# The second FFN product in 20 block products over 4 x 3 x 2 blocks in place of 21 over 2 x 2 x 2

## The chip, the cores and the metric

The kernel runs on one core of a Trainium2 chip, as one program in one launch. Five engines take part, each with its own queue of instructions: TensorE (PE, whose weight loads are shown apart as PEld), VectorE (DVE), ScalarE (ACT), GpSimd (POOL, which does next to nothing here) and SyncE (SP, which issues nearly all DMAs). The metric is the time of the launch on the device in microseconds (us), the median of several runs.

## What is computed

Attention with a sigmoid in place of a softmax, for 8 batches, 12 heads, 448 positions and heads of 64, then a feed-forward network of two products on the joined heads:

```
scores = q @ k.T / sqrt(64) - log(448)
attn   = 1 / (1 + exp(-scores)) @ v            # 8 x 12 x 448 x 64
x      = attn, heads joined                     # 3584 x 768
h      = x @ w_in                               # 3584 x 2048
g      = max(0.01 * h, h)
out    = g @ w_out                              # 3584 x 768
```

All values are float32.

## The kernel before

Rows of x belong to a batch, 448 (S) to each, and two batches (2p and 2p+1) make a pass p; there are four passes (NQ). Results are held transposed: features on the 128 partitions, the 448 positions of one batch along them. Every product of the FFN is done in three matmuls: each operand is split into a high part, which ScalarE rounds to the type that TensorE takes (`copy` into an F32R tile), and a low part, the rest, which VectorE subtracts (`sub`); high x high, high x low and low x high are added up in PSUM.

The work runs in three stages. The first is attention, two heads (a `Pair`) at a time. In it and in the first product a generator, `prep` (line 270), gets the two weight matrices ready on VectorE, a few steps at a time as `prepare(pace)` (line 330) calls for, by the numbers in `PACES` (line 28): it decodes the numbers that come in as int64, forms sums of blocks and stores the results in DRAM tiles `td`. The second stage is the first FFN product (`First`, line 561; slots of nine matmuls, 1.8 us each), the third the second FFN product (the loop at line 795).

Both FFN products use a scheme for 2x2 blocks with seven block products in place of eight: the blocks of the left operand (two batches by two halves of the features) and of the weights (two by two) are added and subtracted beforehand, and each of the seven products (`ORDER`, line 20) goes into one or more of four results. `Quad` (line 158) holds the accumulators and says when one is read out. For the second product the left operands are made at the end of the first: `First.after` (line 586) applies the slope (`leaky`), forms the sums of the four blocks on VectorE (`sums`, three new tiles and one in place for each u, that is, for each of 8 pairs of feature blocks) and stores all seven operands to the DRAM tiles `gd` (`save`).

In the second product the loop runs over items: pass p, product n, and pairs of u (`KS` = 2), so 4 x 7 x 4 = 112 items of 18 matmuls (3 blocks of output columns, 2 u, 3 parts). For item k, in one slot: the weights' tiles, if some are still to be made (load in slot k, high part one slot on, low part two slots on); `g_load(k + 3)`, one DMA of 448 KB; `g_high(k + 2)` on ScalarE; `g_low(k + 2)` on VectorE; and the 18 matmuls of item k. Three buffers hold loaded operands (`gp`, tag `g`) and three the split ones (tag `gs`). Chores that are due (`later`) are issued ahead of the slot's own work: reading an accumulator of a product that has just ended (`collect`, line 789), and the stores of outputs one slot later. The weights' tiles (`Weights`, line 122) are split once, seven of them ahead of the stage (`AHEAD`) and 25 in its first 27 slots; later passes use them again.

The order of the work is written out by hand: `pinned` (line 83) keeps every matmul, DMA, ScalarE and VectorE instruction that goes through it in the order of the program on its queue. The lines that carry it:

```python
def pinned(issue):
    return lambda *args, **kw: tc.keep_in_program_order(issue(*args, **kw))
...
            g_load(k + 3)
            g_high(k + 2)
            g_low(k + 2)
            x = gs.pop(k)[1]
```

In the profile all pinned instructions have line 85, so groups are told apart by their tiles: `px_o`, `py_o`, `pz_o` are accumulators of the second product, `px_h` and so on those of the first, `gg` a loaded operand, `gs` a split one, `wx` and `w` a weight tile before and after its split, `c_o` and `c_h` results, `wd` and `ws` decoded weights and their sums.

Of the kernel before, what the change touches and what calls it, by code (L numbers as in the profile page):

```python
# [25 lines left out]
AHEAD = 7  # L26

PACES = (4, 5, 4.2, 2.8, 2), 2
# [5 lines left out]
LEFT, MORE, RIGHT = 8, 6, 14  # L34

# [16 lines left out]
def attn_ffn_kernel(ctx: ExitStack, tc: tile.TileContext, qk, v, w_in, w_out, out):  # L52
# [21 lines left out]
    NQ = B // 2  # L74
    scale = 1.0 / math.sqrt(D)
# [3 lines left out]
    td = [[tc.dram_tile([P, NOP, HW], F32, name=f"t{w}_{u}") for u in range(NU)] for w in range(2)]  # L79
    xd = [tc.dram_tile([P, NB, S], F32, name=f"xd_{n}") for n in range(4)]  # L80
    gd = [[tc.dram_tile([P, NU, S], F32, name=f"g_{p}_{n}") for n in range(NOP)] for p in range(NQ)]
# [10 lines left out]
    def sub(to, x, y):  # L92
        vec(out=to, in0=x, in1=y, op=ALU.subtract)
# [24 lines left out]
    stage = ctx.enter_context(tc.tile_pool(name="stage", bufs=3))  # L118
# [3 lines left out]
    class Weights:  # L122


        def __init__(self, w, u, g, pool, tag, bufs=None, src=None):
            self.w, self.u, self.g, self.n = w, u, g, len(GROUPS[g])
            self.to = pool, tag, bufs
            self.src, self.stage = src, stage

        def load(self):  # L130
            name = f"wx{self.w}_{self.u}_{self.g}"
            if self.src is None:
                x = self.stage.tile([P, 2, HW], F32, tag="stage", name=name)
            else:
                x = self.src(name).rearrange("p a b -> p (a b)")[:, :2 * HW].rearrange("p (a b) -> p a b", a=2)
            self.x = x[:, :self.n]
            assert (self.w, self.u) in prepared
            dma(out=self.x, in_=td[self.w][self.u][:, PLACES[self.g]])

        def high(self):  # L140
            pool, tag, bufs = self.to
            t = pool.tile([P, 1 if tag == "t1" else 2, 2, HW], F32R, tag=tag, name=f"w{self.w}_{self.u}_{self.g}", bufs=bufs)
            self.t = t[:, :self.n]
            copy(out=self.t[:, :, 0], in_=self.x)
# [4 lines left out]
        def of(self, n):  # L149
            return self.t[:, GROUPS[self.g].index(n)]  # L150

# [68 lines left out]
    left, right = ExitStack(), ExitStack()  # L220

# [47 lines left out]

    def prep():  # L270
# [22 lines left out]
        for at, (m, k) in enumerate(pieces):  # L293
# [22 lines left out]
            dma(out=td[w][u][:, :3], in_=dec[:, 1:])  # L316

            b12, b22, b11, b21 = (dec[:, i] for i in range(4))
            sums = block(F32, (4, HW), f"ws{w}_{u}")
            for to, x, y in ((2, b12, b11), (0, b22, sums[:, 2]), (1, b22, b12), (3, b21, sums[:, 0])):  # L320
                sub(sums[:, to], x, y)
                yield
            dma(out=td[w][u][:, 3:], in_=sums)
# [208 lines left out]
    for p in range(NQ):  # L532
        for u in range(NU):
            for g, members in enumerate(GROUPS):
                w1.append((NOP * (p * NU + u) + ORDER.index(members[0]), Weights(0, u, g, ring, "ring")))
# [25 lines left out]
    class First:  # L561
# [24 lines left out]
        def after(self, quad, c, u, n):  # L586
            got = quad.done(n)
            if got is None:
                return
            p = self.p  # L590
            row, col, t = got
            c[row, col] = t

            def save(n, t):
                dma(out=gd[p][n][:, u], in_=t)

            def sums(n, fn, x, y):
                c[n] = st.tile([P, S], F32, tag="st", name=f"s{n}_{p}_{u}", bufs=ST)
                fn(c[n], c[x], c[y])

            if n != 2:
                later(1, lambda: leaky(t, t))
            if n == 1:
                later(3, lambda: save(0, t))
            elif n == 3:
                later(3, lambda: save(6, t))
            elif n == 6:

                z = LATER if u == NU - 1 else 0
                later(2, lambda: sums(3, add, (1, 0), (1, 1)))  # L610
                later(3 + z, lambda: sums(4, sub, 3, (0, 0)))
                later(4, lambda: save(3, c[3]))
                later(4 + z, lambda: sub(t, c[0, 0], t))
                later(5 + z, lambda: save(4, c[4]))
                later(6 + z, lambda: save(5, t))
            else:
                z = LATER if u == NU - 1 else 0
                later(2, lambda: save(1, t))
                later(4 + z, lambda: sums(2, sub, (0, 1), 4))
                later(6 + z, lambda: save(2, c[2]))  # L620
# [95 lines left out]
    assert next(preps, None) is None  # L716
# [11 lines left out]
    def g_tile(name):  # L728
        return gp.tile([P, KS, S], F32, tag="g", name=name)

    items = [(p, n, u0) for p in range(NQ) for n in ORDER for u0 in range(0, NU, KS)]
    gs = {}

    def g_load(k):
        if k < len(items):
            p, n, u0 = items[k]
            gs[k] = [g_tile(f"gg{p}_{n}_{u0}")]
            dma(out=gs[k][0], in_=gd[p][n][:, u0:u0 + KS])

    def g_high(k):  # L740
        if k < len(items):
            gs[k].append(gp.tile([P, 2, KS, S], F32R, tag="gs", name="gs{}_{}_{}".format(*items[k])))
            copy(out=gs[k][1][:, 0], in_=gs[k][0])

    def g_low(k):
        if k < len(items):
            sub(gs[k][1][:, 1], gs[k][0], gs[k][1][:, 0])

    use = [(g, u) for g in range(len(GROUPS)) for u in range(NU)]
    w2 = {(g, u): Weights(1, u, g, t2a, "t2", None, g_tile) for g, u in use[:AHEAD]}  # L750

    for k in range(NOP, size):
# [8 lines left out]
        if rest == 3:  # L761
            later(0, lambda: g_high(0))
        elif rest == 2:
            later(0, lambda: g_low(0), lambda: g_high(1))
        elif rest == 1:
            later(0, lambda: g_low(1))
        if rest in (7, 6, 5):
            later(0, lambda r=rest: g_load(7 - r))
# [7 lines left out]
    op = ctx.enter_context(tc.tile_pool(name="op", bufs=8, reuse_waits="tile"))  # L776
    t2b = ctx.enter_context(tc.tile_pool(name="t2b", bufs=len(use) - NU - AHEAD - len(GROUPS), reuse_waits="tile"))
    for i, (g, u) in enumerate(use[AHEAD:]):
        one = len(GROUPS[g]) == 1
        pool, tag = (ring, "ring") if i < len(GROUPS) else (t2b, "t1" if one else "t2")  # L780
        w2[g, u] = Weights(1, u, g, pool, tag, NU if one else None)
    psum = banks("ps_o", dict(px=(3, 1), pz=(5, 1)))

    def store(p, m, got):
        row, col, t = got
        b = 2 * p + row
        dma(out=out[col * NB + m, :, b * S:(b + 1) * S], in_=t)

    def collect(p, n, quads):
        for m, x in enumerate(quads):  # L790
            got = x.done(n)
            if got is not None:
                later(1, lambda m=m, got=got: store(p, m, got))

    for k, (p, n, u0) in enumerate(items):
        if u0 == 0:
            if n == ORDER[0]:
                quads = [Quad(psum, op, "o", f"o{p}_{m}", 8) for m in range(NB)]
            accs = [x.into(n) for x in quads]
        g = next(g for g, members in enumerate(GROUPS) if n in members)  # L800
        ending = k == len(items) - 1

        def work():
            for i, step in ((k, "load"), (k - 1, "high"), (k - 2, "low")):
                if 0 <= i < len(use) - AHEAD:
                    getattr(w2[use[AHEAD + i]], step)()
            g_load(k + 3)
            g_high(k + 2)
            g_low(k + 2)
            x = gs.pop(k)[1]  # L810
            for m, (acc, begins) in enumerate(accs):
                for e in range(KS):
                    u = u0 + e
                    parts_mm(acc, w2[g, u].of(n), slice(m * P, m * P + P), x[:, 0, e], x[:, 1, e], begins and u == 0, u == NU - 1)
                if ending and m < NB - 1:
                    store(p, m, quads[m].done(n))
                elif ending:

                    t = op.tile([P, S], F32, tag="o", name="end", bufs=8)
                    b = 2 * p  # L820
                    for cols, how, queue in zip(HALVES, (copy, vcopy), (dma, dma_act)):
                        how(out=t[:, cols], in_=acc[:, cols])
                        queue(out=out[NB + m, :, b * S + cols.start:b * S + cols.stop], in_=t[:, cols])
# [46 lines left out]
```

## Time and profile before

| what | value |
|---|---|
| time of the runs (3) | median 1063.91 us, 1062.86 to 1064.01 |
| time of the profiled execution | 1063.13 us, its span 1061.3 us |
| attention | about 0 to 251 us |
| first FFN product | about 251 to 654 us |
| second FFN product | about 654 to 1058 us |
| granted clock of TensorE | 1.00 |
| HBM | 167.38 MB read, 87.16 MB written |

The profile is of one execution. Its times count from the first instruction, so the time of a launch is somewhat above the span. A busy share is the part of the span in which an engine works on an instruction; waiting at the head of its queue isn't counted. A group of instructions shows what it writes and reads (out<-in), its shape as partitions x elements, how many there are, their busy time and the mean ns of one, and then how long the engine had been idle just before them and what ended the wait. In the order of time a row starts with the start and the duration in us; a wait is put in brackets at its end. Matmuls of 128x448 are listed with some 362 ns because they overlap; what counts is the distance between them.

### The profile page before, as it was taken

How to read it: one execution, taken by the hardware profiler on the slowest of the kernel's cores; microseconds unless marked ns; L12 is line 12 of the kernel's file. 1: busy time of each engine (PE TensorE's matmuls, PEld its weight loads, DVE VectorE, ACT ScalarE, POOL GpSimd, SP SyncE). 2: the span in 40 equal slices, each digit the busy share in tenths (PEclk: the TensorE clock that was granted, in tenths of full speed). 3: DMA queues.
4: the chain of work that ended last, by engine and by line, in shares of the span. 5: the costliest groups of instructions: out<-in, count | busy, mean ns of one | idle time of the engine just before them, and what ended most of it. 6: DMA issues, size and time to landing. Idle time of an engine off the chain costs nothing.

```text
span 1061.3 us, 16140 instructions
## 1 busy us (share of the span) xinstructions
PE 1055.8 (99%) x5882; PEld 889.0 (84%) x5882; DVE 684.2 (64%) x1045; ACT 569.9 (54%) x809; POOL 0.3 (0%) x5
## 2 busy tenths in 40 slices
PE   9999999999999999999999999999999999999998
PEld 5555545557999999998999999999999999999997
DVE  5778989877896898788976666655333433332332
ACT  6877778776555655555565555553323233323331
POOL 0000000000000000000000000000000000000000
PEclk9999999999999999999999999999999999999999
DMA  7878888898798888889788787866554554454542
GB/s 265 284 290 272 289 290 273 281 364 273 229 316 285 242 277 284 299 283 355 241 283 287 256 274 266 319 232 223 169 160 125 178 157 152 130 183 148 160 152 87
DMA packets 107935, 255.61 MB, mean 241 GB/s; under 512 B 11984, under 2 KB 55888, under 8 KB 107856
## 3 DMA queue, kind: packets, MB, share of 16 engines
q1 hardware_dynamic: 107280, 254.02, 72.4%
q8 instruction: 46, 0.75, 0.3%
q10 hardware_dynamic: 576, 0.57, 0.2%
q14 instruction: 33, 0.27, 0.1%
HBM read 167.38 MB, written 87.16 MB: 240 GB/s over the span
## 4 chain that ended last, share of the span: by engine, by line
PE 53%; DVE 0%; ACT 0%; issue 0%
PE px_o L85 22%; PE pz_o L85 11%; PE px_h L85 8%; PE py_o L85 5%; PE pz_h L85 4%; PE py_h L85 2%; DVE end L85 0%; ACT end L85 0%
## 5 line engine op out<-in xcount | busy, mean ns | idle before, releaser
L85 DVE TENSOR_TENSOR gs<-gg,gs 128x896 fp32r<-128x896 f32 x112 | 122.3, 1092 | 226.8 <-ACT gs L85 226.8
L85 PE MATMUL px_o<-gs,w 128*128 128x448 f32 x1152 | 232.5, 362 | 0.0
L85 PE MATMUL px_h<-hi,w 128*128 128x448 f32 x768 | 231.4, 362 | 0.9 <-DVE w L85 0.8
L85 PEld LDWEIGHTS px_o<-gs,w 128*128 128x128 f32 x1152 | 216.0, 187 | 14.4
L85 ACT CAST gs<-gg 128x896 fp32r<-128x896 f32 x112 | 105.3, 941 | 224.4 <-PE px_o L85 116.4
L85 PEld LDWEIGHTS px_h<-hi,w 128*128 128x128 f32 x768 | 143.7, 187 | 11.5 <-DVE w L85 1.6
L85 PE MATMUL px_h<-lo,w 128*128 128x448 f32 x384 | 139.2, 363 | 0.0
L85 DVE TENSOR_TENSOR w<-wx,w 128x768 fp32r<-128x768 f32 (+1 forms) x160 | 136.1, 852 | 4.5 <-ACT w L85 3.9
L85 ACT ACTIVATE s<-sc 128x896 f32<-128x896 f32 x144 | 119.4, 933 | 8.8 <-PE sc L85 8.8
L85 ACT CAST w<-wx 128x768 fp32r<-128x768 f32 (+1 forms) x160 | 119.5, 751 | 8.4 <-DMA wx<-t 8.3
L85 PE MATMUL pz_h<-hi,w 128*128 128x448 f32 x384 | 118.0, 361 | 0.0
L85 PE MATMUL pz_o<-gs,w 128*128 128x448 f32 x576 | 116.5, 362 | 0.0
L85 PEld LDWEIGHTS pz_o<-gs,w 128*128 128x128 f32 x576 | 108.0, 187 | 7.2
L85 PE MATMUL pv<-s,v 128*64 128x448 f32 x576 | 113.8, 543 | 0.0
L85 PEld LDWEIGHTS sc<-qks 64*128 64x128 f32 x876 | 79.4, 185 | 23.8 <-issue 16.9
L85 PE MATMUL sc<-qks 64*128 64x448 f32 (+1 forms) x876 | 95.1, 367 | 0.1
L85 PEld LDWEIGHTS pv<-s,v 128*64 128x64 f32 x576 | 39.1, 137 | 63.3 <-issue 54.1
L85 ACT COPY c_h<-px_h 128x448 f32<-128x448 f32 x64 | 34.1, 534 | 87.9 <-PE px_h L85 87.1
L85 PEld LDWEIGHTS px_h<-lo,w 128*128 128x128 f32 x384 | 72.1, 188 | 5.2
L85 PEld LDWEIGHTS pz_h<-hi,w 128*128 128x128 f32 x384 | 71.9, 187 | 4.6
L85 DVE SCALAR_TENSOR_TENSOR wd<-wr,wd 128x384 int32<-128x384 int32 x128 | 71.3, 557 | 3.2
L85 PE MATMUL pz_h<-lo,w 128*128 128x448 f32 x192 | 69.6, 363 | 0.0
(55 smaller groups left out, 986.0 us busy)
## 6 DMA issues: line engine op xcount, KB each, us to landing
gg<-g SPq DMA_DIRECT2D x112, 448.0 KB, 3.4
wx<-t SPq DMA_DIRECT2D x120, 384.0 KB, 4.4
g<-c_h SPq DMA_DIRECT2D x128, 224.0 KB, 4.5
g<-s SPq DMA_DIRECT2D x96, 224.0 KB, 4.5
qk<-in_qk SPq DMA_DIRECT2D x46, 448.0 KB, 5.4
wr<-in_w_in SPq DMA_DIRECT2D x32, 384.0 KB, 3.4
t<-ws SPq DMA_DIRECT2D x16, 768.0 KB, 6.2
wr<-in_w_out SPq DMA_DIRECT2D x32, 384.0 KB, 4.2
```

The source lines that it names most:

```text
L85: return lambda *args, **kw: tc.keep_in_program_order(issue(*args, **kw))
```

## The change

The second product uses another scheme: rows of the weights in 4 blocks (512 features each, 4 u of 128), output columns in 3 blocks (256 each, 2 of 128) and 2 batches; 20 block products in place of the 24 of the plain way. A block product is now 2 x 4 x 3 = 24 matmuls, and an item is half of one, 12 matmuls; there are 4 x 20 x 2 = 160 items. For each product `PRODUCTS` names the weights' form, an accumulator (a chain, A to E), the left operand, and what is read when it ends: `c` copies the accumulator into an output (ScalarE), `r`, `+` and `-` combine it with one (VectorE), `!` stores the output. A chain isn't cleared between its products, so later reads see running sums. Accumulators have two banks each, four of them.

Left operands: the eight blocks (`RAW`: block 0 to 3, batch 0 or 1) and six sums (`MADE`) are stored in the first product; the others are formed in the second, from two loaded tiles (`g_sum`). Weights: 20 forms are made in `second` (nine VectorE instructions for each u, in place of four) and loaded by `Wide`, three forms to a tile; a tile is loaded straight into the place of its low part. There are 28 tiles, 7 ahead and 21 in the stage. The host orders the blocks of w_out otherwise. The pace of the preparation in the first product goes from 2 to 2.7 steps, and the loaded operands get six buffers in place of three.

```diff
-PACES = (4, 5, 4.2, 2.8, 2), 2
+GG = 6
+PACES = (4, 5, 4.2, 2.8, 2), 2.7
+RAW = "00", "01", "30", "31", "10", "11", "20", "21"
+MADE = {"01+30": "01", "00+30": "00", "10-21": "10", "21-20": "21", "11-10": "11", "11-21": "11"}
+PRODUCTS = (
+    (0, "A", "30", ("c10",)), (2, "B", "21-30", ("c21",)), (1, "A", "01+30", ("c11",)), (3, "B", "21", ("r11",)),
+    (4, "A", "01", ("r21",)), (5, "B", "10-21", ("c01",)), (6, "A", "10+01", ("c20",)), (7, "B", "21-20", ("c00",)),
+    (8, "A", "10", ("r00",)), (9, "B", "20-10", ()), (10, "A", "11-10", ("r01",)), (11, "B", "00+30", ("r10!",)),
+    (12, "D", "01-00", ("-00!",)), (13, "E", "11+01", ()), (14, "C", "30-31", ("-01!", "-21")), (15, "D", "30-20", ()),
+    (17, "C", "01+31", ()), (19, "E", "21-31", ("+21!",)), (18, "D", "10+00", ("-20!",)), (16, "C", "11-21", ("+11!",)))
...
+    class Wide:
+        def load(self):
...
+            dma(out=self.t[:, 1].bitcast(F32), in_=t2d[self.u][:, :, self.forms[0]:self.forms[0] + n])
+        def high(self):
+            copy(out=self.t[:, 0], in_=self.t[:, 1].bitcast(F32))
+        def low(self):
+            sub(self.t[:, 1], self.t[:, 1].bitcast(F32), self.t[:, 0])
...
+    def second(u, dec):
...
+        dma(out=to[:, 7:8], in_=w[:, 0:1])
+        dma(out=to[:, 10:17], in_=w[:, 1:8])
...
+        for fn, to_, x, y in (
+                (add, two(s, 8, 9), at("02", "03"), at("12", "13")), (sub, two(s, 10, 11), at("00", "03"), at("20", "23")),
+                (sub, two(s, 1, 2), two(s, 9, 11), at("10", "22")), (add, two(s, 5, 6), two(s, 8, 10), at("11", "21")),
+                (sub, two(s, 0, 4), at("10", "20"), at("13", "21")), (sub, two(s, 0, 4), two(s, 0, 4), two(s, 2, 1)),
+                (sub, two(s, 3, 7), at("11", "01"), two(s, 2, 6)), (add, s[:, 3], s[:, 3], w[:, BLOCKS.index("12")]),
+                (add, s[:, 7], s[:, 7], s[:, 5])):
+            fn(to_, x, y)
+            yield
+        dma(out=to[:, :7], in_=s[:, :7])
+        dma(out=to[:, 8:10], in_=s[:, 7:9])
+        dma(out=to[:, 17:], in_=s[:, 9:])
...
+            def made(x):
+                fn, (a, b) = (add, x.split("+")) if "+" in x else (sub, x.split("-"))
+                new = st.tile([P, S], F32, tag="st", name=f"s{a}{b}_{p}_{u}", bufs=ST)
+                fn(new, c[a], c[b])
+                later(2, lambda: save(x, new))
...
+            later(2 if n == 2 else 3, lambda: save(name(row, col), t))
+            z = LATER if u == NU - 1 else 0
+            for i, x in enumerate(x for x in MADE if name(row, col) in x and set(x.replace("-", "+").split("+")) <= set(c)):
+                later(2 + i + z, lambda x=x: made(x))
...
+    items = [(p, i, h) for p in range(NQ) for i in range(FORMS) for h in range(2)]
...
     def g_load(k):
...
+        p, i, h = items[k]
+        x = PRODUCTS[i][2]
+        names = [x] if x in gd[p] else operand(x)[1:]
+        mine = []
+        for n in names:
+            if raw.get((p, n, h), -9) < k - 2:
+                t = gp.tile([P, KS, S], F32, tag="g", name=f"g{n[:2]}_{p}_{i}_{h}", bufs=GG)
+                dma(out=t, in_=gd[p][n][:, h * KS:h * KS + KS])
+                raw[p, n, h], gx[p, n, h] = k, t
+                mine.append(n)
+        gs[k] = [None, mine[-1]]
+    def g_sum(k):
...
+        gs[k][0] = gx[p, gs[k][1], h]
+        if x not in gd[p]:
+            fn, a, b = operand(x)
+            fn(gs[k][0], gx[p, a, h], gx[p, b, h])
+            del raw[p, gs[k][1], h]
...
+    def read(p, i):
+        _, chain, _, reads = PRODUCTS[i]
+        acc = accs[p, chain][:, :, :S]
+        for x in reads:
+            how, o = x[0], x[1:3]
+            if how == "c":
+                outs[p, o] = op.tile([P, 2, S], F32, tag="o", name=f"o{p}_{o}")
+                copy(out=outs[p, o], in_=acc)
+            else:
+                t = outs[p, o]
+                a, b = (acc, t) if how == "r" else (t, acc)
+                (add if how == "+" else sub)(t, a, b)
+            if x[3:]:
+                later(1, lambda o=o: store(p, o))
...
+    for j in range(len(use) - AHEAD):
+        loads.setdefault(j * 3 // 2, []).append(w2[use[AHEAD + j]])
     for k, (p, i, h) in enumerate(items):
...
         def work():
-            for i, step in ((k, "load"), (k - 1, "high"), (k - 2, "low")):
-                if 0 <= i < len(use) - AHEAD:
-                    getattr(w2[use[AHEAD + i]], step)()
-            g_load(k + 3)
+            for far, step in ((3, "low"), (2, "high"), (0, "load")):
+                for x in loads.get(k - far, ()):
+                    getattr(x, step)()
+            g_low(k + 1)
+            g_sum(k + 2)
             g_high(k + 2)
-            g_low(k + 2)
-            x = gs.pop(k)[1]
+            g_load(k + 4)
+            x = gs.pop(k)[2]
...
+            for m in range(2):
+                todo = [(e, part, n) for e in range(KS) for part, n in ((0, 0), (0, 1), (1, 0))]
+                for at, (e, part, n) in enumerate(todo):
+                    mm(accs[p, chain][:, m, :S], lhsT=w2[g, h * KS + e].of(form, part, m), rhs=x[:, n, e],
+                       start=begins and at == 0, stop=h == 1 and at == len(todo) - 1, skip_group_check=True)
...
         slot(work)
-        if u0 + KS == NU and not ending:
-            later(0, lambda p=p, n=n, quads=quads: collect(p, n, quads))
+        if h == 1 and not ending:
+            later(0, lambda p=p, i=i: read(p, i))
```

At the very end VectorE adds the last accumulator into its output in halves, where before ScalarE and VectorE copied one half each.

More of the change, by code (lines that the diff above doesn't have):

```diff
@@ L74, in attn_ffn_kernel @@
     NQ = B // 2
+    KQ = NU // 2
     scale = 1.0 / math.sqrt(D)
@@ L268, in attn_ffn_kernel, with firsts, two, at @@
     todo = [(w, u) for w in range(2) for u in range(NU)]
+    def firsts(u, dec):
+        dma(out=td[u][:, :3], in_=dec[:, 1:])
+        b12, b22, b11, b21 = (dec[:, i] for i in range(4))
+        sums = block(F32, (4, HW), f"ws0_{u}")
+        for to, x, y in ((2, b12, b11), (0, b22, sums[:, 2]), (1, b22, b12), (3, b21, sums[:, 0])):
+            sub(sums[:, to], x, y)
+            yield
+        dma(out=td[u][:, 3:], in_=sums)
+    def second(u, dec):
+        to = t2d[u // 2][:, u % 2]
+        w = dec.rearrange("p a b -> p (a b)").rearrange("p (n m) -> p n m", m=P)
+        dma(out=to[:, 7:8], in_=w[:, 0:1])
+        dma(out=to[:, 10:17], in_=w[:, 1:8])
+        s = block(F32, (12, P), f"ws1_{u}")
+        def two(x, i, j):
+            end = j + (1 if j > i else -1)
+            return x[:, i:end if end >= 0 else None:j - i]
+        def at(x, y):
+            return two(w, BLOCKS.index(x), BLOCKS.index(y))
+        for fn, to_, x, y in (
[5 more added lines that the diff above has]
+            fn(to_, x, y)
+            yield
+        dma(out=to[:, :7], in_=s[:, :7])
+        dma(out=to[:, 8:10], in_=s[:, 7:9])
+        dma(out=to[:, 17:], in_=s[:, 9:])
     def prep():
@@ L315, in prep @@
                 continue
[L316 to L323, printed above, removed]
+            if w == 1:
+                yield from second(u, dec)
+            else:
+                yield from firsts(u, dec)
             prepared.add((w, u))
@@ L726, in attn_ffn_kernel, with operand @@
     w1_stage.extend([more.enter_context(tc.tile_pool(name="stage2", bufs=4, side="right", reuse_waits="tile"))])
[L728 to L732, printed above, removed]
-    def g_load(k):
[L735 to L738, printed above, removed]
+    items = [(p, i, h) for p in range(NQ) for i in range(FORMS) for h in range(2)]
+    raw, gx, gs = {}, {}, {}
+    def operand(x):
+        fn = add if "+" in x else sub
+        return (fn, *x.replace("-", "+").split("+"))
+    def g_load(k):
+        if k >= len(items):
+            return
+        p, i, h = items[k]
[10 more added lines that the diff above has]
+    def g_sum(k):
+        if k >= len(items):
+            return
+        p, i, h = items[k]
+        x = PRODUCTS[i][2]
+        gs[k][0] = gx[p, gs[k][1], h]
[3 more added lines that the diff above has]
+            del raw[p, gs[k][1], h]
     def g_high(k):
@@ L742, in g_high @@
             gs[k].append(gp.tile([P, 2, KS, S], F32R, tag="gs", name="gs{}_{}_{}".format(*items[k])))
-            copy(out=gs[k][1][:, 0], in_=gs[k][0])
+            copy(out=gs[k][2][:, 0], in_=gs[k][0])
     def g_low(k):
         if k < len(items):
-            sub(gs[k][1][:, 1], gs[k][0], gs[k][1][:, 0])
-    use = [(g, u) for g in range(len(GROUPS)) for u in range(NU)]
-    w2 = {(g, u): Weights(1, u, g, t2a, "t2", None, g_tile) for g, u in use[:AHEAD]}
+            sub(gs[k][2][:, 1], gs[k][0], gs[k][2][:, 0])
+    use = [(g, u) for g in range(len(TRIPLES)) for u in range(KQ)]
+    w2 = {(g, u): Wide(g, u, t2a, "t2") for g, u in use[:AHEAD]}
     for k in range(NOP, size):
@@ L774, in attn_ffn_kernel @@
     left.close()
[L776 to L777 removed]
+    op = ctx.enter_context(tc.tile_pool(name="op", bufs=6, reuse_waits="tile"))
+    t2b = ctx.enter_context(tc.tile_pool(name="t2b", bufs=len(use) - KQ - AHEAD - len(GROUPS), reuse_waits="tile"))
     for i, (g, u) in enumerate(use[AHEAD:]):
[L779 to L781 removed]
@@ L782, in attn_ffn_kernel @@
[L782 to L800, printed above, removed]
+        small = len(TRIPLES[g]) < 3
@@ new lines, in attn_ffn_kernel, with place, store @@
+        pool, tag = (ring, "ring") if i < len(GROUPS) else (t2b, "t1" if small else "t2")
+        w2[g, u] = Wide(g, u, pool, tag, KQ if small else None)
+    psum = banks("ps_o", dict(acc=(4, 2)))
+    firsts_at = {}
+    for i, (_, chain, _, _) in enumerate(PRODUCTS):
+        firsts_at.setdefault(chain, i)
+    outs, accs = {}, {}
+    def place(p, o):
+        m, t = int(o[0]), int(o[1])
+        b = 2 * p + t
+        return out[2 * m:2 * m + 2, :, b * S:(b + 1) * S]
+    def store(p, o):
+        dma(out=place(p, o).rearrange("m p s -> p m s"), in_=outs[p, o])
@@ L801, in attn_ffn_kernel @@
+    loads = {}
+    for j in range(len(use) - AHEAD):
+        loads.setdefault(j * 3 // 2, []).append(w2[use[AHEAD + j]])
+    for k, (p, i, h) in enumerate(items):
+        form, chain, _, reads = PRODUCTS[i]
+        begins = h == 0 and firsts_at[chain] == i
+        if begins:
+            accs[p, chain] = psum("acc", f"acc{p}_{chain}")
         ending = k == len(items) - 1
         def work():
-            for i, step in ((k, "load"), (k - 1, "high"), (k - 2, "low")):
-                if 0 <= i < len(use) - AHEAD:
-                    getattr(w2[use[AHEAD + i]], step)()
@@ L807, in work @@
-            g_load(k + 3)
-            g_high(k + 2)
-            g_low(k + 2)
-            x = gs.pop(k)[1]
[L811 to L823, printed above, removed]
+            for far, step in ((3, "low"), (2, "high"), (0, "load")):
+                for x in loads.get(k - far, ()):
+                    getattr(x, step)()
@@ new lines, in work @@
+            g_low(k + 1)
+            g_sum(k + 2)
+            g_high(k + 2)
+            g_load(k + 4)
+            x = gs.pop(k)[2]
+            g = form // 3
+            for m in range(2):
[3 more added lines that the diff above has]
+                       start=begins and at == 0, stop=h == 1 and at == len(todo) - 1, skip_group_check=True)
+                if ending:
+                    o, = (x[1:3] for x in reads)
+                    t, acc, to = outs[p, o], accs[p, chain], place(p, o)
+                    for cols, queue in zip(HALVES, (dma, dma_act)):
+                        add(t[:, m, cols], t[:, m, cols], acc[:, m, cols])
+                        queue(out=to[m, :, cols], in_=t[:, m, cols])
```

93 lines of the change are left out of this document (41 added, 52 removed).

## The prediction

> **What bounds the kernel now.** I read the head of the page first, then the chain of waits in order of time, the busy times by stage, the groups with their shapes kept apart, and the order of time around the start of the second product.
>
> ```profile
> span 1061.3 us, 16140 instructions
> PE 1055.8 (99%) x5882; PEld 889.0 (84%) x5882; DVE 684.2 (64%) x1045; ACT 569.9 (54%) x809; POOL 0.3 (0%) x5
> 654.58 14.40 PE px_o L85 x72
> ...
> 1043.38 14.42 PE px_o L85 x72
> ```
>
> The chain ends with 28 such rows, one for each block product of the second FFN product: 72 matmuls of 128x448 in 14.40 us, 0.200 us each, with no gap. The second product is 28 x 72 = 2016 matmuls, 403.2 us, and TensorE alone sets its length. So TensorE work that is left out is time won, but only while the other engines keep up with the shorter slots that remain.
>
> ```profile
> 251.00:654.00 403.00, 402.12 (x2009) 376.22 (x2008) 320.86 (x486) 231.84 (x380) 0.00 (x0) 1.00 0.85 279
> 760.00:1040.00 280.00, 280.00 (x1401) 262.44 (x1401) 98.70 (x102) 89.10 (x111) 0.00 (x0) 1.00 0.50 153
> ```
>
> The columns are the length, then PE, PEld, DVE and ACT busy, POOL, granted clock, DMA share, GB/s. In the first product (251 to 654) VectorE is already 80% busy and TensorE loses 0.9 us in all. In the second, once its weights are split, VectorE is 35% busy and the clock is 1.00: there seems to be much room. What matters is how that room is ordered:
>
> ```profile
> 658.90 0.83 ACT L85 CAST w<-wx 128x768 fp32r<-128x768 f32 x1 [2.39 <-DMA wx<-t]
> 660.84 0.94 ACT L85 CAST gs<-gg 128x896 fp32r<-128x896 f32 x1 [1.11 <-DMA gg<-g]
> 661.82 1.09 DVE L85 TENSOR_TENSOR gs<-gg,gs 128x896 fp32r<-128x896 f32 x1 [2.75 <-ACT gs L85]
> 662.83 0.95 DVE L85 TENSOR_TENSOR w<-wx,w 128x768 fp32r<-128x768 f32 x1
> ...
> 666.15 1.09 DVE L85 TENSOR_TENSOR gs<-gg,gs 128x896 fp32r<-128x896 f32 x1 [2.37 <-ACT gs L85]
> 667.30 0.94 ACT L85 CAST gs<-gg 128x896 fp32r<-128x896 f32 x1 [0.39 <-DVE gs L85]
> ```
>
> Three things are to be seen. First, VectorE takes its instructions in the order of the program and waits at the head: the weight's low part (662.83) had its input at 658.90 + 0.83 = 659.73, yet stood 3.1 us behind the operand's low part, which waited for ScalarE. Second, the hand-overs: ScalarE to VectorE 660.84 + 0.94 = 661.78 to 661.82, 0.04 us; VectorE to ScalarE 666.15 + 1.09 = 667.24 to 667.30, 0.06 us. Third, two VectorE instructions without a wait between them overlap a little: 661.82 to 662.83, so 896 elements hold the engine 1.01 us although the result takes 1.09.
>
> **The change, part by part.**
>
> *TensorE.* Four passes of 20 products, each 24 matmuls of the same 128x448 shape, are 1920. That is 96 fewer: 96 x 0.200 = **-19.2 us**. A slot of the loop (half a product) shrinks from 18 matmuls, 3.6 us, to 12, 2.4 us; in pass p product i takes slots 2i and 2i+1.
>
> *Operands of the second product.* These are the durations:
>
> ```profile
> L85 DVE TENSOR_TENSOR gs<-gg,gs 128x896 fp32r<-128x896 f32 x112 | 122.3, 1092 | 226.8 <-ACT gs L85 226.8
> L85 ACT CAST gs<-gg 128x896 fp32r<-128x896 f32 x112 | 105.3, 941 | 224.4 <-PE px_o L85 116.4 <-PE pz_o L85 68.1 <-PE py_o L85 35.6
> L85 DVE TENSOR_TENSOR w<-wx,w 128x768 fp32r<-128x768 f32 x120 | 113.9, 952 | 3.3 <-ACT w L85 3.3
> L85 DVE TENSOR_TENSOR x<-x,x 128x1344 f32<-128x1344 f32 x8 | 12.4, 1551 | 0.0
> L85 DVE TENSOR_TENSOR s<-c_h,c_h 128x448 f32<-128x448 f32 x32 | 19.9, 621 | 11.3 <-ACT c_h L85 11.3
> L85 DVE TENSOR_TENSOR c_o<-c_o,px_o 128x448 f32<-128x448 f32 x12 | 7.1, 617 | 1.9 <-PE px_o L85 1.9
> ```
>
> Every slot still has one high part on ScalarE (0.94) and one low part on VectorE (1.09). New is that 10 of the 20 products (positions 1, 6, 9 and 12 to 18) take an operand that is not stored: for each of their 20 slots VectorE adds two loaded tiles of 128x896 first. Between the plain f32 rows of 448 (0.62) and 1344 elements (1.55) that is 1.09 us. Eleven times a pass VectorE also takes a 128x896 accumulator into an output; PSUM as an input costs no more (0.617 beside 0.621), so again 1.09. Per pass and without weights that is 40 + 20 + 11 = 71 instructions of 1.01 = 72 us in 40 x 2.4 = 96 us. By the sum alone, VectorE fits.
>
> By its order it does not. In slot k VectorE gets low(k+1), then sum(k+2), and ScalarE high(k+2); in slot k+1 VectorE's next is low(k+2). That one needs high(k+2), which needs the sum just before it. So VectorE stands idle for ScalarE in every slot, with sum(k+3), the reads and the weights' low parts queued behind. One turn of this ring is low 1.01 + sum 1.09 + hand-over 0.06 + high 0.94 + hand-over 0.04 = **3.14 us against the slot's 2.4**: TensorE waits 0.74 us in each slot of a run of sums once the lead is used up. A single read of an accumulator, or a weight's low part, falls into VectorE's 1.04 us of waiting and is free.
>
> The lead differs from run to run. VectorE can't get ahead of a read, since that waits for TensorE to end a product.
>
> ```profile
> 769.62 5.56 PE L85 MATMUL py_o<-gs,w 128*128 128x448 f32 x27
> 769.82 0.53 ACT L85 COPY c_o<-px_o 128x448 f32<-128x448 f32 x1 [0.67 <-PE px_o L85]
> ```
>
> A reader starts 0.2 us after the next product's first matmul. Where a run's first sum shares its slot with such a read (products 1, 6 and 12: reads of 19 of the pass before, 4 and 10), low(k+2) is done at 0.2 + 1.01 + 1.01 + 1.09 + 0.06 + 0.94 + 0.04 + 1.09 = 5.4 us after the slot's start and is wanted at 4.8 + 0.1 (the second matmul reads it): 0.5 us lost in the first slot, 0.74 in the next. Before product 9 stands no VectorE read; the lead of some 1.2 us covers it. Per pass: products 1 and 6, 1.3 each; products 12 to 18, 0.5 + 13 x 0.74 = 10.1; the second of the two reads after product 14, which no longer fits the wait, 0.9. Together 13.6; four passes 54.4; less 1.3, as no read stands before the first pass: **+53 us**.
>
> *Weights in the first pass.* 21 tiles are split in slots 3 to 33, at 0.95 less the overlap = 0.87 us on VectorE, as 25 were before over 25 longer slots. In five slots (10, 18, 22, 24, 30) a low part stands beside a read and no longer fits: five times about 0.8 = **+4 us**.
>
> *Loads.* A pass now loads 52 operand tiles in place of 28.
>
> ```profile
> gg<-g SPq DMA_DIRECT2D x112, 448.0 KB, 3.4
> ```
>
> A load for slot k+4 goes out in slot k, behind low(k+1) at the earliest where its buffer comes free then; in a run of sums its use lies about 6.2 us later, against 3.4 us for one and some 5 for two in a row (SyncE issues one every 0.4 us, and half a DMA share for 153 GB/s means about 1.5 us of all engines for each). I take nothing; if one transfer in the paired stretches came up to 1 us late, about 10 us in all, and that stays in the range.
>
> *First product.* Stored sums fall from 4 to 2 for half of the u and stay 4 for the rest: 32 fewer of 0.53 (one every 0.53 us back to back, 0.62 less the overlap) = -17 us of VectorE. Preparing w_out takes 9 sums in place of 4 per u:
>
> ```profile
> L85 DVE TENSOR_TENSOR ws<-wd x32: 547/552/555, 29.8 to 529.4; 128x384 f32<-128x384 f32 x32
> ```
>
> Seven have 256 elements and two 128; below the 0.55 of this row and above none, at about 0.42 and 0.29 by its neighbours, 3.5 us in place of 2.2 per u, +10 us in all, at 2.7 steps a slot in place of 2. Every issue goes to SyncE as before: 7 stores per u on average, and five t stores in place of two for eight u. VectorE's 82 us of room hide this; without that cover it costs the difference, a few us. I take 0, with -1 (TensorE's present loss) and +5 as bounds. The tail, two adds on VectorE in place of a copy on each of two engines, moves it by under 0.5 us.
>
> *Sum.* The profiled execution took 1063.13 us, 1.8 more than its span: 1063.13 - 19.2 + 53 + 4 = 1101. The median of the runs is 0.8 above the profiled one: **1102 us**.
>
> **The rivals.**
>
> *The ring does not close: faster.* If VectorE had each sum a slot ahead of the low part that follows it (because the built order differs, or the operand tiles give more lead than I see), the turn falls from 3.14 to 1.01 + 1.01 = 2.0 us, plus 0.5 for half a read: about the slot. Then only the double read and the first pass's shared slots cost, 4 x 0.9 + 4 = 8 us at most, and the time is 1064 - 19 + 0 to 8 = 1045 to 1053. For it speaks 72 us of work in 96; against it, the 3.1 us for which a ready low part stood at the head above. It decides from where the loss per slot of sums falls below 19.2 us / 70 slots (18 a pass that are not covered, less the two of the first pass) = 0.27 us.
>
> *The transfers bind: slower still.* The first pass moves 52 + 6 tiles of 0.459 MB and 21 of weights of some 0.38, 34.6 MB; at 153 GB/s / 0.50 = 306 GB/s this takes 113 us, as long as its own ring (96 + 16). If the two add up rather than overlap, the pass grows by 5 to 15 us, the other passes (27 MB, 87 us of 110) by little: 1110 to 1120.
>
> *The clock falls: far slower.* In runs of sums TensorE would stand still for 0.74 us in every 3.14. The granted clock stayed at 1.00 in all windows, also where TensorE lost 0.9 us, but no row shows regular gaps. At half the clock a slot takes 4.8 us, and 14 slots x 1.66 x 4 = 93 us more: 1195. The Trainium skill, TensorE: Matmul & The Clock Gate, in "A second HAM failure mode: psum-queue depth-cycling", says that short idle times between groups of matmuls can make the clock gate swing, which speaks against this change; its table "Why this matters for your kernels" lets gaps under about 3 us pass. By the second the sum stays; the trace can't tell which holds.
>
> *The change doesn't do what it says.* 20 x 24 x 4 follows from the loops, so the matmul count is as good as certain.
>
> **How the numbers follow.** The ring as worked out: 0.80. No ring, 1045 to 1053: 0.10. Transfers: 0.07. Clock: 0.03. The likeliest gives 1102. Its own range: if two slots in three lose the 0.74, 1083; with 10 us of late loads and 5 of the first product, 1117. With the transfers the range is 1078 to 1120; about 15% lies outside, mostly below. A measurement of this kernel tells 0.2%, about 2 us, from no change. Slower than that: 0.88; within: 0.02; faster: 0.10.
>
> **What would show it.** 1920 matmuls in the second product, at 0.200 us where nothing waits; the first product as long as before. In products 12 to 18 the slots come every 3.1 us, with TensorE waiting for VectorE (gs) and VectorE waiting about 1 us for ScalarE (gs) in each; passes of some 110 us, the first some 112. If passes take 96 to 99 us, the ring step is wrong; if TensorE's waits end on a transfer, the step on the loads is; if the second product's stalls lie in products without sums, the count of the lead is.

## The result and the profile after

| | before | changed |
|---|---|---|
| median of the runs | 1063.96 us (4 runs, 1062.86 to 1066.42) | 1113.53 us (4 runs, 1112.84 to 1114.31) |
| span of the profiled execution | 1061.3 us | 1112.5 us |
| second product's first matmul | 654.42 us | 660.59 us |
| second product, first to last matmul's end | 403.4 us | 448.3 us |

The ratio is 1.0463, with a 95% interval of 1.0443 to 1.0482: the change makes the launch 50 us longer, and 45 of them lie in the second product. The forecast was 1102 us in a range of 1078 to 1120.

The head of the page of the changed kernel: fewer matmuls, and VectorE busier by 144 us.

```profile
span 1112.5 us, 16285 instructions
PE 1062.9 (96%) x5786; PEld 867.3 (78%) x5786; DVE 828.1 (74%) x1187; ACT 607.1 (55%) x829; POOL 0.3 (0%) x5
```

Busy times by stage of the changed kernel, for passes 1 and 2 of the second product (columns as before):

```profile
776.00:887.00 111.00, 101.56 (x484) 89.14 (x483) 74.08 (x71) 41.82 (x46) 0.00 (x0) 1.00 0.74 242
887.00:997.00 110.00, 100.62 (x479) 88.20 (x479) 74.08 (x71) 41.94 (x46) 0.00 (x0) 1.00 0.73 240
```

TensorE has 480 matmuls a pass, 96 us of work, and a pass takes 110.4. No engine is full: VectorE has 74 us of work in 110, the DMAs 0.73, the clock is 1.00. An average over the pass shows no bound at all. The order of time in products 16 and 17 of pass 1 shows it:

```profile
862.67 1.09 DVE L103 TENSOR_TENSOR gs<-g,gs 128x896 fp32r<-128x896 f32 x1 [1.09 <-ACT gs L103]
862.95 0.37 PE L103 MATMUL acc_C<-gs,w 128*128 128x448 f32 x1
863.68 1.08 DVE L103 TENSOR_TENSOR g<-g,g 128x896 f32<-128x896 f32 x1
863.82 2.67 PE L103 MATMUL acc_C<-gs,w 128*128 128x448 f32 x12 [0.50 <-DVE gs L103]
864.87 0.94 ACT L103 CAST gs<-g 128x896 fp32r<-128x896 f32 x1 [2.24 <-DVE g L103]
865.85 1.09 DVE L103 TENSOR_TENSOR gs<-g,gs 128x896 fp32r<-128x896 f32 x1 [1.09 <-ACT gs L103]
867.00 2.48 PE L103 MATMUL acc_C<-gs,w 128*128 128x448 f32 x11 [0.51 <-DVE gs L103]
```

One turn is to be followed from row to row. VectorE makes a low part (gs, 862.67), 1.01 us later starts the sum of two loaded tiles (g, 863.68), which ends at 864.76; ScalarE starts the high part at 864.87; it ends at 865.81, and only then, at 865.85, VectorE can make the next low part. That is 3.18 us from low part to low part. TensorE follows at the same distance: its slot starts, does one matmul, and waits for the low part in the second. Both other engines wait within the turn, VectorE 1.09 us for ScalarE and ScalarE 2.24 us for VectorE.

The waits of TensorE in pass 1, and over the launch those of ScalarE and VectorE for each other; the columns are the sum in us, how often, and the longest:

```profile
PE acc_D L103 <- DVE gs L103: 3.7, 6, 1.3
PE acc_E L103 <- DVE gs L103: 2.0, 4, 0.5
PE acc_C L103 <- DVE gs L103: 2.0, 4, 0.5
PE acc_A L103 <- DVE gs L103: 0.9, 2, 0.5
PE acc_B L103 <- DVE gs L103: 0.9, 2, 0.5
```

```profile
ACT gs L103 <- DVE g L103: 199.9, 77, 5.5
DVE gs L103 <- ACT gs L103: 88.8, 88, 2.1
```

In pass 1 all of TensorE's waits end on a low part, none on a transfer, and 14 of 18 are in the accumulators C, D and E, that is, in products 12 to 18 with their sums in a row (some of the gap is shown at the weight load before, so these rows hold less than the 14.4 us that the pass lost).

### The profile page after: what moved, and what is told of

Read it like the earlier page. It is cut to its first block, busy times and chain, and to the rows that moved or that the text cites. A ratio compares the mean times of both kernels' runs of the same rounds, so it can differ in the third digit from the quotient of the medians.

```text
span 1112.5 us, 16285 instructions
## 1 busy us (share of the span) xinstructions
PE 1062.9 (96%) x5786; PEld 867.3 (78%) x5786; DVE 828.1 (74%) x1187; ACT 607.1 (55%) x829; POOL 0.3 (0%) x5
## 4 chain that ended last, share of the span: by engine, by line
PE 69%; DVE 16%; ACT 6%; issue 6%; DMA 1%; ACTq 0%; DVEq 0%; SPq 0%
PE px_h L103 18%; PE pv L103 11%; PE sc L103 10%; PE pz_h L103 9%; PE acc_A L103 8%; DVE g L103 7%; PE acc_B L103 6%; ACT gs L103 6%; DVE gs L103 5%; PE py_h L103 4%; PE acc_C L103 2%; DVE w L103 1%; DMA wx<-t 1%; DVE s L103 1%; PE acc_D L103 1%
## 5 line engine op out<-in xcount | busy, mean ns | idle before, releaser
L103 ACT CAST gs<-g 128x896 fp32r<-128x896 f32 x160 | 149.0, 942 | 242.0 <-DVE g L103 199.9
L103 DVE TENSOR_TENSOR gs<-g,gs 128x896 fp32r<-128x896 f32 x160 | 172.6, 1089 | 89.7 <-ACT gs L103 88.8
L103 PE MATMUL acc_B<-gs,w 128*128 128x448 f32 x576 | 122.2, 364 | 4.8 <-DVE gs L103 4.8
L103 PE MATMUL acc_A<-gs,w 128*128 128x448 f32 x576 | 121.6, 364 | 4.8 <-DVE gs L103 4.8
L103 PEld LDWEIGHTS acc_B<-gs,w 128*128 128x128 f32 x576 | 107.1, 188 | 16.0 <-DVE gs L103 8.9
L103 PEld LDWEIGHTS acc_A<-gs,w 128*128 128x128 f32 x576 | 107.2, 187 | 15.4 <-DVE gs L103 8.2
L103 DVE TENSOR_TENSOR w<-wx,w 128x768 fp32r<-128x768 f32 (+1 forms) x128 | 109.0, 853 | 6.2 <-ACT w L103 6.2
L103 ACT CAST w<-wx 128x768 fp32r<-128x768 f32 (+1 forms) x128 | 95.9, 750 | 0.3
L103 DVE TENSOR_TENSOR g<-g,g 128x896 f32<-128x896 f32 x80 | 86.8, 1085 | 0.0
L103 PE MATMUL acc_D<-gs,w 128*128 128x448 f32 x288 | 67.5, 377 | 16.1 <-DVE gs L103 16.1
```

## The experiments

From the order of time, the start of each pass (its first matmul on accumulator A behind the last on C) gives a table of the second product; "start" is its first matmul, and the last pass is counted to 0.200 us after the start of its last matmul. The launch is the median of 4 runs for the changed kernel and of 9, 10 and 8 runs for the last three versions; every other version was run once. The kernel before took 1063.5 to 1064.0 us each time it was measured beside them.

| version | launch us | start | pass 0 | pass 1 | pass 2 | pass 3 |
|---|---|---|---|---|---|---|
| changed kernel | 1113.53 | 660.59 | 115.8 | 110.45 | 110.4 | 111.5 |
| adds left out | 1058.69 | 658.75 | 102.75 | 96.9 | 96.85 | 97.9 |
| one load, adds kept | 1112.06 | 658.44 | 115.8 | 110.4 | 110.4 | 111.5 |
| sum ahead of low part | 1094.94 | 660.64 | 111.9 | 105.8 | 105.8 | 105.3 |
| sums on GpSimd | 1119.9 | 660.25 | 125.9 | 108.5 | 109.3 | 110.1 |
| sum ahead, reads behind | 1073.95 | 659.51 | 106.9 | 100.15 | 99.85 | 101.9 |
| two more stored, order as changed | 1087.47 | 662.19 | 109.1 | 103.0 | 103.3 | 104.0 |
| preparation spread | 1110.38 | 656.49 | 115.8 | 110.5 | 110.5 | 111.5 |
| sum ahead, reads behind, two more stored | 1067.28 | 664.48 | 103.55 | 97.4 | 98.2 | 99.9 |
| the same, preparation spread | 1063.23 | 656.87 | 104.2 | 97.4 | 97.4 | 98.3 |
| the same, earlier second low part | 1061.10 | 656.65 | 102.1 | 98.4 | 98.2 | 98.9 |

### The adds alone, and the loads alone

The theory is the ring; the rival is the 52 loads a pass in place of 28. Two kernels take one away and leave the other. The first leaves the additions out:

```diff
         if x not in gd[p]:
             fn, a, b = operand(x)
-            fn(gs[k][0], gx[p, a, h], gx[p, b, h])
             del raw[p, gs[k][1], h]
```

> The sums of two loaded operands in the second product are left out (the 80 additions on VectorE); both tiles are still loaded, so transfers, splits, reads and matmuls stay; the output is another. Ring theory (each low part waits for ScalarE's high part, which waits for the sum just before it on VectorE): without the sum a turn is about 2 us, under the slot's 2.4, so the later passes fall from 110.4 to 96 to 98 us, the first from 116 to 100 to 106, and the launch from 1113.5 to 1055 to 1067 us. Transfer theory (52 loads of 448 KB a pass in place of 28 hold the slots): passes stay at 108 us or more, launch 1105 to 1114.

Measured: 1058.69 us, passes of 96.9 and a first of 102.75. Pass 1 of this kernel, all but its last microseconds:

```profile
sum 90.00, PE 89.42 PEld 83.50 DVE 50.14 ACT 39.16 POOL 0.00; mean PE 89.42 PEld 83.50 DVE 50.14 ACT 39.16 POOL 0.00
```

TensorE is busy 89.4 of 90 us, with all 208 loads of operands still there. The 80 additions, 87 us of VectorE's work, cost 55 us of the launch although VectorE stood idle for 36 us of every pass. This kernel takes away the ring and some of VectorE's work at once; the versions below that keep all the work and change its order tell the two apart.

The second keeps the additions and loads one tile of each pair:

```diff
-                dma(out=t, in_=gd[p][n][:, h * KS:h * KS + KS])
                 raw[p, n, h], gx[p, n, h] = k, t
                 mine.append(n)
+        dma(out=gx[p, mine[-1], h], in_=gd[p][mine[-1]][:, h * KS:h * KS + KS])
...
-            fn(gs[k][0], gx[p, a, h], gx[p, b, h])
+            fn(gs[k][0], gs[k][0], gs[k][0])
```

> Where an operand is the sum of two tiles only one is loaded, and it is added to itself; so a pass has 40 operand loads in place of 52, and the 80 additions stay; the output is another. Ring theory: the later passes stay at 109.5 to 110.5 us, the first falls from 116 to 112 to 114, launch 1108 to 1113. Transfer theory: the stretches with pairs of loads speed up, passes of 96 to 102 us, launch under 1085.

Measured: 1112.06 us, and passes that agree with the changed kernel's to 0.1 us, the first too; I had expected 2 to 4 us less there. DMA issues of the two, loaded operands only, the changed kernel first:

```profile
g<-g SPq DMA_DIRECT2D x208, 448.0 KB, 4.2
```

```profile
g<-g SPq DMA_DIRECT2D x160, 448.0 KB, 4.2
```

48 loads less change nothing in the second product, so the operands' transfers are hidden behind the ring, also in the first pass.

### Opening the ring

If the ring is the cause, its order can be changed with all the work kept. One line moves:

```diff
-            g_low(k + 1)
             g_sum(k + 2)
             g_high(k + 2)
+            g_low(k + 1)
             g_load(k + 4)
```

> One change of order: in each slot VectorE takes the sum for two slots ahead before the low part for the next slot, so that ScalarE makes the high part of that sum while VectorE works on the low part. Ring theory: the ring of 3.14 us opens, but low parts now stand behind a read of an accumulator and a sum, and a load has some 2.7 us from its issue to its use in place of 6.2; later passes of 104 to 109 us in place of 110.4, the waits no longer VectorE for ScalarE but VectorE for loads and TensorE for a late low part; launch 1090 to 1108. Transfer theory: no gain, 1110 or above.

Measured: 1094.94 us, later passes of 105.3 to 105.8, as the ring theory had it and not the transfer theory. VectorE's waits in pass 1:

```profile
DVE gs L103 <- ACT gs L103: 12.5, 11, 2.1
DVE g L103 <- DMA g<-g: 5.5, 5, 2.7
```

Its waits for ScalarE have halved (25 us a pass before), and it now waits for loads, as its sums stand earlier in each slot. A low part still stands behind a read and a sum in its slot. So the reads were moved behind it too:

```diff
             g_low(k + 1)
+            while ended:
+                read(*ended.pop())
             g_load(k + 4)
...
         if h == 1 and not ending:
-            later(0, lambda p=p, i=i: read(p, i))
+            ended.append((p, i))
```

> The swap of the sum and the low part, and besides VectorE's and ScalarE's reads of an accumulator moved behind the low part in their slot. Ring theory: the low part no longer stands behind a read as well; what is left is late loads in the stretches with pairs. Later passes of 101 to 103 us in place of 105.8 with the swap alone, the first 105 to 110; launch 1076 to 1086.

Measured: 1073.95 us, passes of 100, slightly better than expected. Order alone, with the same instructions, has taken 40 of the 50 us back.

### The sums on another engine

```diff
+    pvec = pinned(nc.gpsimd.tensor_tensor)
...
-        fn = add if "+" in x else sub
+        fn = padd if "+" in x else psub
```

> The 80 sums go to GpSimd, which did nothing, with all else in the same order; VectorE keeps low parts and reads. Ring theory: VectorE no longer has the sum ahead of the low part. If GpSimd takes under 2.4 us for 128x896, the later passes take 96 to 98 us, the first 100 to 107, launch 1055 to 1068; if it takes 3.5 us, the runs of 14 sums last as long as GpSimd, about 15 us a pass more. Transfer theory: passes stay at 108 us or more.

Measured: 1119.9 us, slower than the changed kernel, and against my expectation: a sum takes GpSimd 2.34 us on average, under 2.4, yet the later passes took 108.5 to 110.1 us and didn't fall to 98. Taken alone, that is what the transfer theory had said. The groups of this kernel:

```profile
L103 DVE TENSOR_TENSOR gs<-g,gs 128x896 fp32r<-128x896 f32 x160 | 236.3, 1497 | 86.5 <-ACT gs L103 86.0
L103 POOL TENSOR_TENSOR g<-g,g 128x896 f32<-128x896 f32 x80 | 186.9, 2343 | 914.7 <-DMA g<-g 900.9 <-DVE gs L103 10.3 <-DVE w L103 2.3
```

VectorE's low part took 1.50 us on average in place of 1.09. The order of time shows why:

```profile
835.64 1.09 DVE L103 TENSOR_TENSOR gs<-g,gs 128x896 fp32r<-128x896 f32 x1 [0.28 <-ACT gs L103]
837.80 2.13 POOL L103 TENSOR_TENSOR g<-g,g 128x896 f32<-128x896 f32 x1 [11.45 <-DMA g<-g]
838.04 2.84 DVE L103 TENSOR_TENSOR gs<-g,gs 128x896 fp32r<-128x896 f32 x1 [1.31 <-ACT gs L103]
840.58 2.29 POOL L103 TENSOR_TENSOR g<-g,g 128x896 f32<-128x896 f32 x1 [0.66 <-DMA g<-g]
841.86 1.09 DVE L103 TENSOR_TENSOR o<-acc_A,o 128x896 f32<-128x896 f32 x1 [0.99 <-PE acc_A L103]
```

A low part took 1.09 us alone (835.64) and 2.84 us beside a sum (838.04); a read, which has one of its inputs in PSUM, took 1.09 us beside the next one (841.86). The same holds over the whole second product: low parts that stand alone in the order of time, with no sum beside them, took 1.08 or 1.09 us, low parts beside a sum up to 3.04, and reads beside a sum 1.07 to 1.09. So the sum left VectorE's queue but slowed it. The Trainium skill, GPSIMD Engine Reference, in "1. Specifications", says that GpSimd shares its SBUF interfaces with VectorE and contends, among others, with VectorE instructions that have two SBUF inputs; a low part is one and a read isn't, and these rows agree. The slower low part is shown; that it alone sets the length of these passes is not. GpSimd needn't wait for a low part before its next sum, and in the order of time it waits for loads between its sums (0.66 us ahead of 840.58), while SyncE's issues of loads wait for low parts and sums that give their buffers back (in pass 1 for 47.4 and 22.8 us). How much of the 108.5 us, and of the longer first pass (125.9), is due to slow low parts, and how much to loads that wait for buffers, was not taken apart.

### The length of the runs

The prediction counted 0.5 us for a run's first slot and 0.74 for each further one. Two more operands stored in the first product (four sums for every u) cut the run of 14 into 4, 2 and 4, with VectorE's order as in the changed kernel:

```diff
-MADE = {"01+30": "01", "00+30": "00", "10-21": "10", "21-20": "21", "11-10": "11", "11-21": "11"}
+MADE = {"01+30": "01", "00+30": "00", "10-21": "10", "21-20": "21", "11-10": "11", "11-21": "11", "30-31": "31", "01+31": "31"}
```

> The changed kernel with two more operands (30-31 and 01+31) stored in the first product and nothing else: VectorE's order is as in the changed kernel, but the run of 14 slots of sums becomes runs of four, two and four. Ring theory: 0.74 us for each slot of a run after the lead; later passes of 102 to 103.5 us, the first 106 to 109; launch 1080 to 1087. If the loss were one of VectorE's total work alone, 4 sums of 71 instructions less would give 4 us a pass: passes of 106, launch 1095 to 1100.

Measured: 1087.47 us, later passes of 103.0 to 104.0: 7.1 to 7.5 us less in passes 1 and 2 for four sums less a pass (4.0 us of VectorE), as the count by runs says, and not as VectorE's total says. The launch came out 0.5 us above what was expected, as the first product took 411.4 us in place of 408.1, with four sums for every u.

### The first product

It took 408.1 us (252.47 to 660.59) in place of 404.8 (249.63 to 654.42). TensorE's waits for a weight's low part in it, before and after:

```profile
PEld px_h L85 <- DVE w L85: 1.6, 2, 1.2
```

```profile
PEld px_h L103 <- DVE w L103: 5.5, 8, 1.7
```

The test keeps the work and spreads it:

```diff
-PACES = (4, 5, 4.2, 2.8, 2), 2.7
+PACES = (4, 5, 4.2, 2.8, 2), 1.55
...
-        go(todo, first.step, PACES[1] * (7 <= k < size - 7 and k % 7 in (6, 0, 1, 2)))
+        go(todo, first.step, PACES[1] * (7 <= k < size - 7))
```

> The same steps of the weights' preparation in the first product, spread over all seven slots of a u (1.55 a slot) in place of four of them (2.7 a slot). Theory: the 3.3 us that the first product lost (TensorE waiting for a weight's low part on VectorE, eight times) come from bursts of preparation ahead of that low part; spread out, the waits fall from eight to under four and the first product takes 405 to 407 us in place of 408.1. Rival: they come from VectorE's total work (more steps, larger sums); then the waits stay at 3 us or more. The second product stays at 448 us; launch 1108 to 1113.

Measured: 1110.38 us, three such waits of 2.3 us in all, the first product 406.1 us (250.37 to 656.49). So bursts of 2.7 steps a slot ahead of a low part in VectorE's queue make up 2 of the 3.3 us; VectorE's busy time in this stage had even fallen, from 322 us before to 315. The other 1.3 us were not taken apart.

### A version that gains

Both changes of order (the version at 1073.95 us) and the two stored operands put together:

> As the last one, and two more operands (30-31 and 01+31) are stored in the first product, four sums for every u, so that the run of 14 slots of sums becomes runs of four, two and four. Ring theory with loads: no run is long enough to use up the lead; later passes of 96 to 97 us, the first 99 to 106; the first product as long as in the changed kernel, 408 us, or up to 3 us more. Launch 1055 to 1066, the ratio to the kernel before 0.992 to 1.002.

Measured: 1067.28 us, ratio 1.0030 (1.0016 to 1.0044), above what was expected. The first pass (103.55) is in its range; the later ones took 97.4 to 99.9 us against 96 to 97, and the first product took 412.0 us against 408 to 411: it has four sums for every u on top of the bursts.

Then the preparation was spread as well:

> As the last one, with the preparation spread over all seven slots of a u. If bursts are what the first product loses, 1 to 3 us less than without the spread: launch 1053 to 1063. If VectorE's total work is, no difference.

Measured: 1063.23 us, ratio 0.9993 (0.9977 to 1.0008), just above the expected range and no difference from the kernel before. The spread is worth 4 us here, more than expected; the first product took 406.3 us. What was left at the start of the second product was a wait for the second low part, behind the last sums to be stored:

```diff
-            later(0, lambda: g_low(0), lambda: g_sum(1), lambda: g_high(1))
+            later(0, lambda: g_low(0), lambda: g_sum(1), lambda: g_high(1), lambda: g_low(1))
```

(with the first five loads one slot earlier, and both steps left out of the first slot of the loop).

> As the version with the swap, the late reads, the two stored sums and the spread preparation, and the second item's low part is made in the last slot of the first product, ahead of the last sums that are stored, with the first loads one slot earlier. That version lost 2.2 us of TensorE in front of that low part at the start of the second product. Ring theory: the wait at the start falls to under 1 us; launch 1059 to 1062, ratio to the kernel before 0.995 to 0.999. If the first operands' loads come late instead, the wait stays and the ratio is 0.999 to 1.001.

Measured: 1061.10 us, ratio 0.9979 with an interval of 0.9968 to 0.9991: 2.4 us, or 0.2%, under the kernel before, and in the expected range. TensorE's wait at the start fell to 0.9 us. The first pass fell by 2.1 us, of which products 0 and 1 are 1.1; the other 1.0 us lies in products 14 to 17, where the version before had a fall of the clock and this one had none. The later passes came out 0.6 to 1.0 us longer than in the version before it, for which I have no reason that was tested.

## Why the prediction was right, and where it was off

*The ring.* Confirmed in its mechanism by the two kernels that separate adds from loads and by the two that keep all the work and change its order, and in its size by the rows: 3.18 us a turn against 3.14 forecast. The 0.04 comes from the hand-over to ScalarE, 0.11 us here (864.76 to 864.87) where the row before showed 0.06. Passes 1 and 2 were worked out as 96 + 13.6 = 109.6 us and took 110.45 and 110.4; 14 slots x 0.04 is 0.6 of that difference.

*TensorE's saving.* 1920 matmuls at 0.200 us, as forecast: without the adds the products of pass 1 take 4.80 us each but for product 15, which takes 5.66 with the second of two reads ahead of it, together 96.9 us.

*The lead and the runs.* In pass 1 products 1, 6 and 12 lost 1.4 us each (forecast 1.3, 1.3 and 1.24), product 9 nothing, as forecast, and products 13 to 18 lost 1.55 to 1.57 us each (forecast 1.48), but for product 15, which lost 2.39 with the double read (forecast 2.4). Confirmed too by the kernel with two more operands stored: 103.0 and 103.3 us in passes 1 and 2, where the count by runs had given 102 to 103.5.

*The first pass.* The term that was too small: 96 + 12.3 + 4.1 = 112.4 forecast, 115.8 measured. The weights' shared slots were right: products 5, 9, 11 and 12 took 0.71 to 0.84 us longer than in pass 1, and 15 and 16 together 0.66, in all 3.7 of the 4.1 us. The pass isn't held by operands' loads, as the kernel with fewer of them shows. Besides the ring's own excess, two things were missing. At the start the second low part stood behind the last four stored sums, and product 0 took 1.5 us longer than in pass 1:

```profile
664.58 2.48 PE L103 MATMUL acc_A<-gs,w 128*128 128x448 f32 x11 [1.24 <-DVE gs L103]
```

And the 1.3 us that were taken off, as no read stands before the first pass, were lost all the same: product 1 took 6.27 us, as in pass 1 (6.21). After the late start the low parts followed each other at about the ring's spacing from the first (663.44, 666.54, 669.72), so there was no lead; without the adds product 1 took 4.80 us behind the same start.

The clock fell once in this pass, which I had priced only as a case for all passes:

```profile
750.19 3.75 PE L103 MATMUL acc_D<-gs,w 128*128 128x448 f32 x11 [1.92 <-DVE gs L103]
```

```profile
750.00:754.00 4.00, 3.81 (x12) 3.42 (x13) 3.52 (x5) 0.94 (x1) 0.00 (x0) 0.63 0.70 223
```

(rows of the order of time of the changed kernel and of its busy times by stage). After a gap of 1.9 us in product 15 eleven matmuls took 3.75 us in place of 2.48, with a granted clock of 0.63. These 1.3 us were not lost for good: VectorE's ring went on meanwhile, and product 16 took 5.19 us where it took 6.36 in pass 1.

*The clock as a rival.* In passes 1 to 3 TensorE has a gap of about 0.8 us in every 3.18 us through products 12 to 18, and the windows show 1.00. So regular gaps of this size don't bring the clock down here, and the swing that the Trainium skill, TensorE: Matmul & The Clock Gate, describes in "A second HAM failure mode: psum-queue depth-cycling" is not seen. The Trainium skill's table "Why this matters for your kernels" on the same page warns of gaps over about 3 us only; here the clock fell after gaps of 1.92 us in the changed kernel and in three of the others, and yet stayed at 1.00 after gaps of 2.12 and 2.24 us in the kernel with the sum ahead, and of 2.23 us in two versions with more operands stored. So the length of one gap doesn't decide alone; what else does was not tested.

*The transfers as a rival.* Refuted as the cause: 48 loads less left the time as it was. They do become what VectorE waits for once the ring is open.

*No ring.* Refuted: VectorE's order on the chip is that of the program.

*The first product.* Taken at 0 with a bound of +5, measured +3.3. The step that failed is that VectorE's 82 us of room hide the preparation: the room is there, but not ahead of the low part that TensorE waits for.

*The tail.* Forecast at under 0.5 us. TensorE waited 0.8 us for the add of the last accumulator's first half before it wrote the second, which makes up most of the 1.1 us that pass 3 took beyond pass 2.

*The sum.* Forecast: -19.2 + 57 = +38. Measured between the two profiled spans: 51.2 us, of which the second product is 44.9 (6.9 over the forecast: 3.4 in the first pass, 0.8 in each of the next two, 1.9 in the last), the first product 3.3, and attention 2.8. Of the last, 2.5 us had come up within the first 12.5 us: the first 30 matmuls of the scores took 4.05 us in place of 2.54, and the next eight 1.77 in place of 1.13, at a granted clock of 1.00 in both. In the other kernels with this same stage the 30 took 2.7 to 4.05 us, and in the one with fewer loads the first product began at 249.63 as in the kernel before, so I don't count these to the change; what sets them stays open.

## What to carry to other kernels

A busy share doesn't say whether an engine has room: it is the order of an in-order queue that decides. Where engine A makes x, engine B turns x into y, and A's next instruction needs y, A stands idle for B in every turn, however empty both look; one instruction of another slot put between the two opens the ring, and here that was worth 19 us with one line and 40 with two. Before fewer matmuls are bought with more work elsewhere, write out the queue of the engine that gets that work for two neighbouring slots, and add up the turn.

## What the runs showed of the hardware beyond this

A GpSimd addition of two 128x896 tiles takes 2.34 us on average, and a VectorE subtraction with both inputs in SBUF that runs beside it up to 3.04 us in place of 1.09, while a VectorE instruction of the same size with one input in PSUM stays at 1.09. TensorE's granted clock fell after some single gaps of 1.9 to 2.3 us (to 0.63 over four microseconds in the changed kernel) and not after others of 2.1 to 2.2; it fell after the one of 2.9 us (the kernel with both orders, two more operands stored and the preparation spread, where 23 matmuls after the gap took 6.47 us in place of some 4.9) and the one of 4.7 us (the kernel with the sums on GpSimd, 0.50). Gaps of 0.8 us in every 3.2 us, and all single gaps of up to 1.7 us, left it at 1.00.
